# Induced attention with a running maximum in three of four batches, a one-product quadrant sum, and a rearranged first phase

## The chip, the cores and the metric

The kernel runs on one core of a Trainium2 chip. The metric is device time in microseconds for one execution. The kernel before has a median of 840.47 us over three runs (840.34 to 840.56).

Five engines matter. TensorE (PE in the profile; PEld is its weight load) multiplies and writes to the accumulator banks. VectorE (DVE) and ScalarE (ACT) read banks, compute elementwise and write to the on-chip memory. GpSimd (POOL) here does mostly one kind of subtraction. SyncE (SP) issues the transfers. Each engine works through its own instructions in the order in which they are written.

## The reference, cut to what matters

```python
B, N, m, C = 4, 12544, 32, 128          # batches, tokens, inducing points, channels
def mab(q, kv):                         # attention of q over kv
    s = scale * (q @ kv.transpose(0, 2, 1))
    a = np.exp(s - s.max(-1, keepdims=True))
    a /= a.sum(-1, keepdims=True) + 1e-09
    return a @ kv
h   = mab(inducing, x)                  # 32 x 128 per batch: "first attention"
y   = mab(x, h)                         # 12544 x 128 per batch: "second attention"
out = max(y @ w1, y @ w2, y @ w3) @ w_out   # 128 -> 768 -> 128, per token
```

All arrays are f32. The first attention reduces over all 12544 tokens of a batch, so h of a batch is known only after its last token.

## The kernel before, in words

A batch's 12544 tokens are 98 tiles of 128. They are worked in seven groups: group 0 has 2 tiles, groups 1 to 6 have 16 each. A full group is again four chunks of 512 tokens.

**First attention of a group.** `attend_products` (L265) forms the scores with the inducing points, 32 rows in each of four partition quadrants, in a bank. `attend_max` (L275), `attend_column` (L282), `attend_spread` (L289) and `attend_least` (L293) find the group's maximum per inducing point and leave its negative in column `gi` of `mneg`. `attend_weights` (L299) takes the exponential, with the row sums in column `gi` of `lst`. `attend_transpose` (L313) turns the weights, `attend_sums` (L323) multiplies them with the tokens, again in four column quadrants, and `attend_keep` (L336) copies the 128 x 128 result into slot `gi` of `hg`. So each group has its own maximum, and seven partial results lie in `hg`.

**Joining the groups.** After the last group `combine_least`, `combine_weights` and `combine_mask` (L401, L406, L411) make a weight per group; `combine_groups` (L422) multiplies each of the seven slots of `hg` by a masked selection matrix, which adds groups and quadrants; `sum_groups` and `total_sums` (L432, L434, L438) do the same for the sums of the exponentials; `invert_total` (L442, L443) and `combine_states` (L448) give `hT`, the scaled h.

**From h to the weights of the chunk loop.** Since y = p @ h (p are the second attention's weights), y @ w can be had as p @ (h @ w). U = h @ wcat, 32 x 1664, is formed once per batch. In batches 1 to 3 `combine_products` (L489) does this in two halves, each with 64 columns of TensorE twice; `combine_high` and `combine_low` split the result into a rounded part and its remainder, and `combine_rows` (L509) moves them with four transfers into the rows of `us`. In batch 0 `first_products`, `first_high` and `first_low` (L462, L467, L473 to L478) do it another way.

**The chunk loop.** A slot is one chunk and one of six 128-column blocks of the 768. `advance` issues pu (L605) and pv (L611) for a coming slot, the relu on ACT (L620), the rounded part hi on ACT (L627), the remainder lo on POOL or DVE (L635, L641) and the maximum h on DVE (L638). `stage2`, six slots behind, issues three products per slot into the accumulator (L661 to L663) and a fourth at a chunk's start (L660). A plain slot so has five TensorE products of 512 columns, and a window of 24 slots is one group.

**Order.** Everything is hand-ordered: each engine's instructions run in the order in which the Python statements issue them. The first attention and the second attention's scores (L524) of the next group or batch are put into the loop by a plan: `at(s, f)` calls f in slot s. In each window two `burst` calls, in slots 2 and 15, issue the quadrant products together. The first attention of batches 1 to 3 runs inside the chunk loop of the batch before. The first attention of batch 0 has nothing to hide under: it is `phase1_first`, into which the conversion of the weights is cut (`work(n)` takes n further steps of `convert`, L161 to L190, mostly on DVE; `WORK` says how many per group). Then the string `ORDER` sets the steps up to the chunk loop: a and b are softmax steps of the first two groups, a digit k is `first_high` of piece k, c is `first_low` of that piece, s is `advance`.

## Time and profile before

| what | value |
|---|---|
| median of three runs | 840.47 us |
| the profiled execution | 838.86 us, of it 837.0 us span, mean granted TensorE clock 0.996 |
| TensorE busy | 815.4 us, 97% of the span |
| ScalarE, VectorE, GpSimd busy | 741.9, 629.9, 635.3 us |
| TensorE busy, 0 to 50 us | 37.9 us |
| TensorE busy, 260 to 430 us (batch 1's loop) | 169.41 of 170 us |
| TensorE busy, 630 to 800 us (batch 3's loop, no first attention beside it) | 169.99 of 170 us |
| last TensorE product ends | about 833.4 us |

The span is from the first to the last instruction; the difference to the execution's own time lies around the program. Rows of the timeline give the start and the duration of an instruction or of a run of like ones (x8: eight of them); products are pipelined, so a product of 512 columns is listed with 0.39 us, while the next starts 0.23 us later. What an insertion costs is therefore read from starts, not from durations. An f32 product is two matmul instructions, a product in the rounded format is one. Idle time before an instruction, with what ended it, stands in square brackets.

### The profile page before, as it was taken

The numbers are of one execution on the slowest core, as the hardware profiler recorded it, in microseconds if no ns is written. First come the engines' busy times: TensorE is split into PE (matmuls) and PEld (weight loads), VectorE is DVE, ScalarE is ACT, GpSimd is POOL, SyncE is SP. The second block draws the span as 40 slices with busy tenths as digits, with TensorE's granted clock in tenths as the row PEclk, the third lists the DMA queues.
The fourth block names the chain that finished last, engine by engine and source line by source line (L and its number), as shares of the span: only waits on it lengthen the run. The fifth ranks groups of instructions, "written<-read, shape, count | busy, mean of one in ns | idle before, by whom it ended". The sixth has DMA issues, their size and how long they took to land.

```text
span 837.0 us, 14668 instructions
## 1 busy us (share of the span) xinstructions
PE 815.4 (97%) x4608; PEld 636.5 (76%) x4608; DVE 629.9 (75%) x1076; ACT 741.9 (89%) x1547; POOL 635.3 (76%) x512
## 2 busy tenths in 40 slices
PE   6879999999999999999999999999999999999998
PEld 4647777777788777877778778777778878778786
DVE  4958787778687777877777878777868778777864
ACT  5759898898799988988889989889879999999996
POOL 0049788787598787886878978878759888888887
PEclk9989999999999999999999999999999999999999
DMA  9823624433435345244333362431232222222221
GB/s 351 305 85 122 221 73 160 172 107 114 134 87 173 124 161 171 73 157 154 127 92 127 113 223 72 161 123 55 64 90 75 74 76 73 67 64 76 73 79 51
DMA packets 42717, 102.50 MB, mean 122 GB/s; under 512 B 8976, under 2 KB 11152, under 8 KB 37392
## 3 DMA queue, kind: packets, MB, share of 16 engines
q1 hardware_dynamic: 42640, 101.57, 37.4%
q8 instruction: 37, 0.61, 0.3%
q14 instruction: 40, 0.33, 0.1%
HBM read 48.12 MB, written 25.69 MB: 88 GB/s over the span
## 4 chain that ended last, share of the span: by engine, by line
PE 92%; DVE 1%; issue 0%; ACT 0%; DVEq 0%; ACTq 0%
PE acc L661 17%; PE pu L605 16%; PE pv L611 16%; PE acc L662 16%; PE acc L663 16%; PE acc L660 3%; PE aux L524 3%; PE acc L323 2%; PE aux L265 2%; PE aux L489 1%; PE aux L422 1%; DVE h L638 0%; PE acc L289 0%; DVE lo L641 0%; DVE rec L443 0%
## 5 line engine op out<-in xcount | busy, mean ns | idle before, releaser
L635 POOL TENSOR_TENSOR lo<-h,hi 128x512 fp32r<-128x512 f32 (+1 forms) x498 | 629.4, 1296 | 146.3 <-ACT hi L627 90.0
L638 DVE TENSOR_TENSOR h<-pv,ru 128x512 f32<-128x512 f32 (+1 forms) x600 | 404.4, 675 | 182.4 <-PE pv L611 117.1
L620 ACT ACTIVATE ru<-pu 128x512 f32<-128x512 f32 (+1 forms) x600 | 375.4, 626 | 66.8 <-PE pu L605 63.7
L627 ACT CAST hi<-h 128x512 fp32r<-128x512 f32 (+1 forms) x600 | 386.6, 644 | 0.3 <-DVE h L638 0.3
L661 PE MATMUL acc<-hi,wo_hi 128*128 128x512 f32 (+1 forms) x600 | 237.9, 396 | 0.0
L605 PE MATMUL pu<-pT,us 128*128 128x512 f32 (+1 forms) x600 | 233.2, 389 | 2.8 <-DVE us L473 1.0
L611 PE MATMUL pv<-pT,us 128*128 128x512 f32 (+1 forms) x600 | 233.3, 389 | 0.0
L662 PE MATMUL acc<-hi,wo_lo 128*128 128x512 f32 (+1 forms) x600 | 231.8, 386 | 0.0
L663 PE MATMUL acc<-lo,wo_hi 128*128 128x512 f32 (+1 forms) x600 | 231.6, 386 | 0.0
L661 PEld LDWEIGHTS acc<-hi,wo_hi 128*128 128x128 f32 x600 | 113.1, 188 | 43.0 <-issue 21.8
L605 PEld LDWEIGHTS pu<-pT,us 128*128 128x128 f32 x600 | 113.5, 189 | 26.2 <-POOL us L478 2.1
L611 PEld LDWEIGHTS pv<-pT,us 128*128 128x128 f32 x600 | 113.7, 189 | 23.6 <-DVE h L638 1.2
L663 PEld LDWEIGHTS acc<-lo,wo_hi 128*128 128x128 f32 x600 | 112.9, 188 | 23.0
L662 PEld LDWEIGHTS acc<-hi,wo_lo 128*128 128x128 f32 x600 | 113.0, 188 | 20.6
L641 DVE TENSOR_TENSOR lo<-h,hi 128x512 fp32r<-128x512 f32 x102 | 72.5, 711 | 0.8 <-ACT hi L627 0.8
L668 ACT COPY o<-acc 128x512 f32<-128x512 f32 (+1 forms) x100 | 61.6, 616 | 3.1 <-PE acc L663 3.1
L660 PE MATMUL acc<-pT,us 128*128 128x512 f32 (+1 forms) x100 | 38.9, 389 | 0.0
L221 POOL TENSOR_TENSOR wo_lo<-wf,wo_hi 128x768 fp32r<-128x768 f32 x1 | 1.8, 1817 | 40.5 <-ACT wo_hi L220 40.5
L323 PEld LDWEIGHTS acc<-xg,aT 128*32 128x32 f32 x768 | 20.4, 110 | 12.6 <-ACT ru L620 5.7
L265 PE MATMUL aux<-xT,iT 128*32 128x512 f32 x192 | 25.9, 596 | 2.1 <-ACT xT L257 2.1
L323 PE MATMUL acc<-xg,aT 128*32 128x128 f32 x768 | 25.8, 274 | 0.4
L524 PE MATMUL aux<-xT,hT 128*32 128x512 f32 x192 | 25.6, 604 | 0.0
(104 smaller groups left out, 438.2 us busy)
## 6 DMA issues: line engine op xcount, KB each, us to landing
out_dram<-o SPq DMA_DIRECT2D x96, 256.0 KB, 2.0
xg<-in_x_dram SPq DMA_DIRECT2D x23, 1024.0 KB, 6.9
xT<-in_xt_dram SPq DMA_DIRECT2D x18, 1024.0 KB, 5.6
pT<-ph SPq DMA_DIRECT2D x192, 64.0 KB, 2.0
pT<-pl SPq DMA_DIRECT2D x192, 64.0 KB, 2.0
raw<-in_w_dram SPq DMA_DIRECT2D x3, 768.0 KB, 12.1
us<-uh SPq DMA_DIRECT2D x6, 208.0 KB, 3.1
us<-ul SPq DMA_DIRECT2D x6, 208.0 KB, 3.7
```

The source lines that it names most:

```text
L323: nc.tensor.matmul(out=hps[q * M : (q + 1) * M, :C], lhsT=aT[:, t * M : (t + 1) * M], rhs=xg[:, t, :], start=(t < NQ), stop=(t + NQ >= nt),)
L605: nc.tensor.matmul(out=pu[:, :w], lhsT=state[c.b]["us"][:, 2 * j * P : (2 * j + 1) * P], rhs=c.pT[:, :w], start=True, stop=True)
L611: nc.tensor.matmul(out=pv[:, : d.w], lhsT=state[d.b]["us"][:, (2 * j + 1) * P : (2 * j + 2) * P], rhs=d.pT[:, : d.w], start=True, stop=True,)
L620: nc.scalar.activation(out=ru[:, :w], in_=pu[:, :w], func=AF.Relu)
L627: nc.scalar.copy(out=hi[:, : c.w], in_=h[:, : c.w])
L635: nc.gpsimd.tensor_sub(**args)
L638: nc.vector.tensor_max(out=h[:, : d.w], in0=pv[:, : d.w], in1=relus.pop(s)[:, : d.w])
L641: nc.vector.tensor_sub(**low)
L660: nc.tensor.matmul(out=c.acc[:, :w], lhsT=us[:, 2 * DF :], rhs=c.pT[:, :w], start=True, stop=False)
L661: nc.tensor.matmul(out=c.acc[:, :w], lhsT=wo_hi[:, j, :], rhs=c.hh[j][:, :w], start=False, stop=False)
L662: nc.tensor.matmul(out=c.acc[:, :w], lhsT=wo_lo[:, j, :], rhs=c.hh[j][:, :w], start=False, stop=False)
L663: nc.tensor.matmul(out=c.acc[:, :w], lhsT=wo_hi[:, j, :], rhs=c.hl[j][:, :w], start=False, stop=(j == NJ - 1))
```

## The change

1. **Running maximum and sums in batches 1 to 3.** `attend_least` takes the smaller of the group's column of `mneg` and the one before. The new `attend_scale` (ScalarE) makes the factor exp(old maximum - new maximum), `al`. The new `attend_add` (VectorE) does hs = hs * al + h, 128 x 128, and the same for the sums, 128 x 1. The copy into `hg` stays for group 0 only, and the weights, the mask and the seven-fold product go. Batch 0 keeps the way it had.
2. **One product for the quadrants.** `add_quadrants` is one f32 product of `hs` with the selection matrix, 32 columns, beside `total_sums`.
3. **U in four column groups at once.** `combine_products` is four products of 416 columns, each with 32 columns of TensorE, into one bank; there is one `combine_high` and one `combine_low` of 128 x 416, and `combine_rows` is sixteen transfers of 32 x 416, four at a time, three slots apart.
4. **Weighted sums last in a burst.** `attend_sums` is issued behind `attend_products`.
5. **First phase.** The inducing points' load is the first on the queue and their scaling the first on ScalarE; four conversion steps instead of two stand ahead of the loop over groups, and two fewer behind the last group's minimum; the w2 transposes and the products from them come one group earlier; the joining is written in another order; and `ORDER` has `c` earlier in two places.

```diff
-    WORK = ((2, 2), (2, 2), (2, 2), (3, 2), (3, 2), (0, 3))
-    ORDER = "a a a a b a a b 0 c m b a a b a b p b 1 s b b b c s S m b 2 s c s 3 c s"
+    WORK = ((2, 2), (2, 2), (2, 2), (3, 2), (3, 2), (1, 0))
+    ORDER = "a a a a b a a b 0 c m b a a b a b p b 1 s c b b b s S m 2 b s c 3 c s s"
 ...
     def attend_least(b, gi):
         nc.vector.tensor_reduce(out=st["mneg"][:, gi : gi + 1], in_=st["mp"][:, :NQ], axis=AX.X, op=ALU.min)
+        if b > 0 and gi > 0:
+            nc.vector.tensor_tensor(
+                out=st["mneg"][:, gi : gi + 1], in0=st["mneg"][:, gi : gi + 1], in1=st["mneg"][:, gi - 1 : gi], op=ALU.min
+            )
 ...
+    def attend_scale(b, gi):
+        st = state[b]
+        st["al"] = wk.tile([P, 1], F32, name="al", tag="al")
+        nc.scalar.activation(out=st["al"], in_=st["mneg"][:, gi - 1 : gi], func=AF.Exp,
+                             bias=st["mneg"][:, gi : gi + 1], scale=-1.0)
+    def attend_add(b, gi):
+        st = state[b]
+        if gi == 0:
 ...
+            nc.scalar.copy(out=st["hs"][:parts, :], in_=st["h"][:parts, :C])
+            st["l1"] = st["lst"][:, :1]
+            return
+        for total, new in ((st["hs"], st["h"][:, :C]), (st["l1"], st["lst"][:, gi : gi + 1])):
+            nc.vector.scalar_tensor_tensor(
+                out=total, in0=total, scalar=st["al"], in1=new, op0=ALU.mult, op1=ALU.add
+            )
+    def add_quadrants(st, bank):
+        st["sum"] = bank
+        nc.tensor.matmul(out=bank[:, :M], lhsT=st["hs"], rhs=sel[:, :M], start=True, stop=True)
 ...
     def phase1_first(weights):
         start_batch(0)
+        nc.sync.dma_start(out=iT, in_=ind_t)
+        nc.scalar.mul(out=iT, in_=iT, mul=scale)
         first_loads()
 ...
-        work(2)
+        work(4)
 ...
-            if gi == NG - 2:
+            if gi == NG - 3:
                 transpose_w2()
+            if gi == NG - 2:
+                prep_products()
 ...
+        attend_weights(0, NG - 1)
         attend_sums(0, NG - 2, bank_o[1])
         attend_keep(0, NG - 2)
-        attend_weights(0, NG - 1)
         combine_least(state[0])
         combine_weights(state[0])
         attend_transpose(0, NG - 1)
-        prep_products()
 ...
+    def combine_products(st, bank):
 ...
+        for k in range(NQ):
+            nc.tensor.matmul(out=bank[k * M : (k + 1) * M, :UQ], lhsT=st["hT"][:, :M],
+                             rhs=wcat[:, k * UQ : (k + 1) * UQ], start=True, stop=True)
 ...
-                    first += [(attend_sums, n, g - 1), (attend_products, n, g, bank_a[1])]
-                    at(s0 + 3, attend_keep, n, g - 1)
+                    first += [(attend_products, n, g, bank_a[1]), (attend_sums, n, g - 1)]
+                    at(s0 + 3, attend_add, n, g - 1)
 ...
-                    at(s0 + 10, combine_least, ("state", n))
-                    at(s0 + 11, combine_weights, ("state", n))
-                    at(s0 + 14, combine_mask, ("state", n))
-                    at(s0 + 16, attend_keep, n, g + 1)
-                    at(s0 + 15, sum_groups, ("state", n))
+                    at(s0 + 16, attend_add, n, g + 1)
+                    at(s0 + 18, add_quadrants, ("state", n), bank_a[1])
                     at(s0 + 18, total_sums, ("state", n), bank_a[0])
-                    at(s0 + 17, combine_groups, ("state", n), range(NG), bank_a[1])
                     at(s0 + 19, invert_total, ("state", n))
-                    at(s0 + 20, combine_states, ("state", n), 2)
-                    at(s0 + 21, combine_products, ("state", n), 0, bank_a[0])
-                    at(s0 + 21, combine_products, ("state", n), 1, bank_a[1])
+                    at(s0 + 19, combine_states, ("state", n), 1)
+                    at(s0 + 21, combine_products, ("state", n), bank_a[0])
 ...
+                    for r in range(NQ):
+                        at(s0 + 25 + 3 * r, combine_rows, ("state", n), r)
```

Three places of the order. First TensorE, where batch 1's groups are joined (hs is the running sum, sel the selection matrix, lst and l the sums of the exponentials). Before:

```order
L611 MATMUL pv_84<-pT,us 128x512
L422 MATMUL aux_80<-sw,hg 128x64 x7
L661 MATMUL acc_85<-hi,wo_hi 128x512
L662 MATMUL acc_85<-hi,wo_lo 128x512
L663 MATMUL acc_85<-lo,wo_hi 128x512
L605 MATMUL pu_82<-pT,us 128x512
L611 MATMUL pv_83<-pT,us 128x512
L438 MATMUL aux_79<-sel,l_2633 128x32
L660 MATMUL acc_86<-pT,us 128x512
```

Now, one slot later than the seven products stood:

```order
L639 MATMUL pu_82<-pT,us 128x512
L645 MATMUL pv_83<-pT,us 128x512
L372 MATMUL aux_80<-sel,hs 128x32
L477 MATMUL aux_79<-sel,lst 128x32
L694 MATMUL acc_86<-pT,us 128x512
```

Seven products of 64 columns have gone; one of 32 columns stands beside the one for the sums. U's products (L489 before, L524 now) stand three slots after L438 in both.

Second, VectorE at the end of batch 0's first attention (t, pw, rest, dst and wcat are conversion steps, mq and mneg the last group's maximum). Before:

```order
L275 TENSOR_REDUCE mq<-aux_79 128x1
L313 STREAM_TRANSPOSE aT<-a 128x512
L293 TENSOR_REDUCE mneg<-acc_85 128x1
L185 SCALAR_TENSOR_TENSOR dst<-size,rest 128x768
L190 TENSOR_TENSOR wcat<-dst,wf 128x6x128
L401 TENSOR_REDUCE mmin<-mneg 128x1
```

Now:

```order
L183 SCALAR_TENSOR_TENSOR dst<-size,rest 128x768
L188 TENSOR_TENSOR wcat<-dst,wf 128x6x128
L276 TENSOR_REDUCE mq<-aux_79 128x1
L319 STREAM_TRANSPOSE aT<-a 128x512
L294 TENSOR_REDUCE mneg<-acc_85 128x1
L440 TENSOR_REDUCE mmin<-mneg 128x1
```

The last two conversion steps stand ahead of the last group's maximum; two steps that stood behind group 1's maximum now stand ahead of it.

Third, ScalarE between the first attention and the chunk loop (uf is a copy from which POOL forms the remainder of piece 1 of U, ph the rounded weights of the first full group). Before:

```order
L467 CAST us<-acc_86 128x512
L620 ACTIVATE ru<-pu_81 128x256
L567 CAST ph<-aux_80 128x512
L477 COPY uf<-acc_86 64x512
L620 ACTIVATE ru<-pu_82 128x256
```

Now:

```order
L506 CAST us<-acc_86 128x512
L654 ACTIVATE ru<-pu_81 128x256
L516 COPY uf<-acc_86 64x512
L601 CAST ph<-aux_80 128x512
L654 ACTIVATE ru<-pu_82 128x256
```

The copy uf has moved ahead of ph.

More of the change, by code (lines that the diff above doesn't have):

```diff
@@ L106 @@
     iT = const.tile([P, M], F32, name="iT")
-    nc.sync.dma_start(out=iT, in_=ind_t)
     def load_raw(src):
@@ L141 @@
     nc.gpsimd.memset(eps, 1e-9)
-    nc.scalar.mul(out=iT, in_=iT, mul=scale)
     wf = xtp.tile([P, 2, DF], F32, name="wf", tag="xT")
@@ L478, in first_low @@
         nc.gpsimd.tensor_sub(out=us[low], in0=uf[low, :n], in1=us.bitcast(F32)[low])
[L481 to L488 removed]
+    def combine_products(st, bank):
+        st["us"] = bp.tile([P, UW], F32R, name="us", tag="us")
+        st["up"] = bank
+        for k in range(NQ):
             nc.tensor.matmul(
[L490 to L492 removed]
+                out=bank[k * M : (k + 1) * M, :UQ],
+                lhsT=st["hT"][:, :M],
+                rhs=wcat[:, k * UQ : (k + 1) * UQ],
                 start=True,
@@ L715, in softmax1 @@
         at(s + 8 + wait, attend_weights, b, gi)
+        if gi > 0:
+            at(s + 9 + wait, attend_scale, b, gi)
         at(s + 10 + wait, attend_transpose, b, gi)
```

83 lines of the change are left out of this document (41 added, 42 removed).

## The prediction

> **What bounds the kernel now.** First the page's busy times, then four stretches: the stall before the chunk loop (50 to 70 us), batch 1's loop, batch 3's loop.
>
> ```profile
> PE 815.4 (97%) x4608; PEld 636.5 (76%) x4608; DVE 629.9 (75%) x1076; ACT 741.9 (89%) x1547; POOL 635.3 (76%) x512
> ...
> 50.00:60.00 10.00, 5.88 (x27) 4.05 (x27) 6.45 (x14) 6.34 (x18) 3.99 (x6) 0.76 0.24 57
> 60.00:70.00 10.00, 10.00 (x56) 8.19 (x55) 8.32 (x15) 9.24 (x21) 7.84 (x8) 0.89 0.71 243
> 260.00:430.00 170.00, 169.41 (x990) 130.78 (x989) 128.40 (x219) 151.75 (x317) 132.82 (x105) 1.00 0.43 138
> 630.00:800.00 170.00, 169.99 (x778) 136.18 (x777) 134.81 (x223) 162.93 (x330) 144.63 (x116) 1.00 0.25 73
> ```
>
> The columns are length, then busy time of TensorE, its weight load, VectorE, ScalarE and GpSimd, the granted clock and DMA. In both loops TensorE is busy practically all the time. Batch 3's row has no first attention beside it; there ScalarE fills 162.93 of 170 us and TensorE still does not wait. So in batches 0 to 2, where ScalarE fills 151.75, a microsecond taken from TensorE should be a microsecond of the total. Before about 60 us it is otherwise: TensorE idles there, and waits decide.
>
> **U in four column groups.** The timeline's TensorE rows around U's products in batch 1's preparation, and around a burst of one kind in batch 3:
>
> ```profile
> 217.58 0.39 PE L611 MATMUL pv<-pT,us 128*128 128x512 f32 x1
> 218.42 1.62 PE L489 MATMUL aux<-wcat,hT 128*64 128x416 f32 x8 [0.45 <-DVE hT L448]
> 220.30 0.40 PE L662 MATMUL acc<-hi,wo_lo 128*128 128x512 f32 x1
> ...
> 686.23 0.39 PE L605 MATMUL pu<-pT,us 128*128 128x512 f32 x1
> 686.46 0.39 PE L611 MATMUL pv<-pT,us 128*128 128x512 f32 x1
> 686.77 1.06 PE L524 MATMUL aux<-xT,hT 128*32 128x512 f32 x8
> 688.11 0.39 PE L662 MATMUL acc<-hi,wo_lo 128*128 128x512 f32 x1
> ```
>
> A plain step is 0.23 us (686.23 to 686.46), and from L611 to L662 there are two, 0.46. The old insertion therefore costs 220.30 - 217.58 - 0.46 = 2.26 us, with the wait for hT in it. Eight matmul instructions in four column groups of 512 columns cost 688.11 - 686.46 - 0.46 = 1.19 with both changes of column width. The new ones have 416 columns; eight of 512 take 0.89 (124.08 to 124.97 below), so 96/512 of that, 0.17, comes off: 1.02. The saving is 1.24 per batch, 3.7 us for three. Bounds: 1.07 (no scaling) to 1.24, and 0.5 less if hT is late again. I take it as not late: the steps that make hT stand one slot earlier, and the mask (L411) ahead of them is gone. The Trainium skill's TensorEngine Tiling (Array Packing), section Theoretical Speedup, gives up to 2x for a dimension of 64 and 4x for 32; by that the 1.62 would become 0.81 and the saving would be about 0.1 us smaller per batch, which leaves the sum where it is within its bounds.
>
> **One product for the quadrants.**
>
> ```profile
> 210.97 0.39 PE L611 MATMUL pv<-pT,us 128*128 128x512 f32 x1
> 211.21 1.67 PE L422 MATMUL aux<-sw,hg 128*128 128x64 f32 x14
> 213.00 0.40 PE L662 MATMUL acc<-hi,wo_lo 128*128 128x512 f32 x1
> 213.70 0.39 PE L611 MATMUL pv<-pT,us 128*128 128x512 f32 x1
> 213.93 0.30 PE L438 MATMUL aux<-sel,l 128*128 128x32 f32 x2
> 214.38 0.39 PE L661 MATMUL acc<-hi,wo_hi 128*128 128x512 f32 x1
> ```
>
> The fourteen instructions cost 213.00 - 210.97 - 0.46 = 1.57 us, the sums' pair 214.38 - 213.70 - 0.46 = 0.22. Two such pairs side by side should cost 0.44 (bounds 0.22, if the second hides, to 0.9, if hs is late by what hT was). Saving 1.57 + 0.22 - 0.44 = 1.35 per batch, 4.0 us. hs is written in slot 16, on VectorE, and read in slot 18.
>
> **Weighted sums last.** The two burst forms, the transpose between them, and the weight loads' waits for the whole run:
>
> ```profile
> 92.50 1.07 PE L524 MATMUL aux<-xT,hT 128*32 128x512 f32 x8
> 92.78 0.71 DVE L313 STREAM_TRANSPOSE aT<-a 128x512 f32<-128x512 f32 x1
> 93.64 1.08 PE L323 MATMUL acc<-xg,aT 128*32 128x128 f32 x32
> ...
> 124.08 1.07 PE L524 MATMUL aux<-xT,hT 128*32 128x512 f32 x8
> 124.97 1.06 PE L323 MATMUL acc<-xg,aT 128*32 128x128 f32 x32
> ...
> PEld acc L323 <- ACT ru L620: 5.7, 6, 0.9
> ```
>
> At 92.50 the sums start 1.14 us after the scores, at 124.08 only 0.89: 0.25 is lost where aT ends at 93.49, just before they can start. The last row counts six such places (it names ScalarE, which had long been done; it is the transpose). With the products of about 0.87 between, aT is ready. That gives 1.5 us; bounds 0 (the wait appears elsewhere) and 1.5. Order inside a burst changes no other cost that these rows show.
>
> **What comes in its place, and its cover.**
>
> ```profile
> L448 DVE TENSOR_TENSOR hT<-pu,rec 128x128 f32<-128x128 f32 x1 | 0.3, 292 | 0.1
> L293 DVE TENSOR_REDUCE mneg<-acc 128x1 f32<-128x4 f32 x28 | 4.3, 153 | 1.2 <-PE acc L289 1.2
> 216.57 0.58 SPq L590 DMA_DIRECT2D pT<-pl  x1
> ```
>
> Per group, eighteen times in all, VectorE gets a 128 x 128 update from a bank (nearest 0.29), a 128 x 1 update and a 128 x 1 minimum (nearest 0.15 each): 0.6 us, at most 10.8 us altogether, while it idles 41.6 of 170 us in batch 1's loop. Behind them on VectorE stands the next h, for which POOL, ScalarE and pv's bank wait; the pipeline is six slots long, so I charge nothing. ScalarE exchanges a copy for a small exponential. SP issues sixteen transfers for U instead of four, about 0.58 each, 7 us more per batch in groups of four; behind them stand the p transfers of the next chunks. Their last four are issued in slot 34, and `us` is first read about thirteen slots (17 us at 1.3) later: hidden.
>
> So the loops give 3.7 + 4.0 + 1.5 = 9.2 us (bounds 6.5 to 9.9).
>
> **The first phase.** Rows of the timeline:
>
> ```profile
> 6.13 0.44 PE L265 MATMUL aux<-xTs,iT 128*32 128x64 f32 x8 [2.45 <-ACT iT L143]
> 13.09 0.69 DVE L275 TENSOR_REDUCE mq<-aux 128x1 f32<-128x512 f32 x1 [3.58 <-PE aux L265]
> 25.79 1.09 PE L255 MATMUL pu<-ident,xg 128*128 128x128 f32 x8 [0.68 <-DMA xg<-in_x_dram]
> 29.01 1.06 PE L265 MATMUL aux<-xT,iT 128*32 128x512 f32 x8
> 31.73 0.68 DVE L275 TENSOR_REDUCE mq<-aux 128x1 f32<-128x512 f32 x1
> 38.45 0.16 DVE L293 TENSOR_REDUCE mneg<-acc 128x1 f32<-128x4 f32 x1 [0.19 <-PE acc L289]
> 40.39 0.15 DVE L401 TENSOR_REDUCE mmin<-mneg 128x1 f32<-128x7 f32 x1
> 45.54 0.32 PE L524 MATMUL aux<-xTs,hT 128*32 128x64 f32 x8 [0.59 <-DVE hT L448]
> ...
> 53.03 0.58 ACT L567 CAST ph<-aux 128x512 fp32r<-128x512 f32 x1 [0.91 <-DVE aux L564]
> 53.64 0.58 ACT L477 COPY uf<-acc 64x512 f32<-64x512 f32 x1
> 54.27 0.49 PE L462 MATMUL acc<-wcat,hT 128*128 128x128 f32 x2 [1.34 <-ACT uf L477]
> 55.61 0.58 PE L605 MATMUL pu<-pT,us 128*128 128x256 f32 x1 [0.85 <-POOL us L478]
> ```
>
> The earlier load of iT takes up to 2.45 us out of the start, but group 5's tokens arrive at 25.79, and TensorE had waited 0.68 for them already: most of the gain is spent in a longer wait there. What remains is VectorE's lateness. Group 5's scores end at 30.07, its maximum starts at 31.73; two conversion steps moved into the hole of 3.58 let VectorE be on time: 1.5 us, less about 0.4 because one more step now stands between groups 5 and 6, and 0.2 for arrival: 0.9 (bounds 0 to 1.5). Then mmin started 1.94 us after the last group's minimum, with two steps between; it now follows at once, but the exponential and transpose of the last group are next late, so I take 1.4 (bounds 0 to 1.94). Third, uf goes ahead of ph, which waited 0.91: it gains about 1.5, TensorE's wait of 1.34 goes, POOL's remainder and with it L605 come 1.5 sooner, and the second `c` moved helps a little: 1.8 (bounds 0, if the next wait takes it all, to 2.1). First phase 4.1, bounds 0 to 5.5.
>
> Sum: 9.2 + 4.1 = 13.3. The profiled execution took 838.86, which becomes 825.6 (span 837.0 to about 823.7); the median of the runs is 840.47, which becomes **827.2**.
>
> **Rivals.**
>
> *The first phase gives almost nothing*: data arrive as before, and the waits between 46 and 60 us close up differently. 25.79 with its wait speaks for it; the 3.58 hole and ph's wait against. 840.47 - 9.2 = 831.3.
>
> *The granted clock stays up.* In 50 to 70 us the clock averages 0.76 and 0.89, which is 2.4 + 1.1 = 3.5 us of TensorE time. It falls after idle stretches (5.88 busy of 10). If the shortened waits keep it at 1.00, up to 3 us more come: 840.47 - 13.3 - 3 = 824.2. Against it: waits of about 1 us remain there. The Trainium skill, TensorE: Matmul & The Clock Gate, section What's actually happening, says that a window of about 3.4 us judged idle halves the clock and that the window runs freely; by that the outcome depends on where the waits fall in it, and a longer low stretch is as possible as none.
>
> *ScalarE sets the pace after all* in batches 0 to 2, and TensorE's savings become its idle time: only the first phase counts, 840.47 - 4.1 = 836.4. Batch 3's row speaks against it.
>
> *VectorE's running update costs a slot.* The update stands in VectorE's queue between two h; if the next pv must wait for h there, each of eighteen groups loses time. It decides from 13.3/18 = 0.74 us per group on; at a whole slot, 1.3 us, it costs 23.4: 840.47 - 13.3 + 23.4 = 850.6. Against it stand VectorE's idle quarter and the six slots.
>
> That the change does not do what it says is excluded by the order of the instructions: the fourteen are gone, the column groups are there.
>
> **How the numbers follow.** The forecast gets 0.60, the empty first phase 0.14, the clock 0.13, ScalarE's pace 0.08, VectorE's slot 0.05. The range 823 to 832 holds the first three and the bounds of the sum; above it lie the last two. A measurement of this kernel can tell 0.2% (1.7 us) from no change. Faster by more: 0.92; within: 0.03; slower: 0.05.
>
> **What would show it.** Right: no L489-like wait for hT, U's insertion near 1.0 us and the joining near 0.44 from start to start, no wait of the sums' weight loads, the last minimum of batch 0 near 37.5, and the scores L524 near 43.2. Wrong: TensorE idle for h or ru in batches 0 to 2, a new wait for `us` at a batch's start, or a gain in the first phase that is gone again by 62 us.

## The result, and the profile after

The kernel after takes 834.85 us (median of four runs, 834.19 to 836.23), the kernel before 840.51 beside it (840.34 to 840.72). The ratio is 0.9935, with a 95% interval of 0.9917 to 0.9952. So it is 5.7 us faster where 13.3 were forecast: the direction holds, the size does not, and the time lies above the range.

The page of after, then the same stretches as before in the view of windows (length, then busy time of TensorE, weight load, VectorE, ScalarE, GpSimd, the granted clock, DMA):

```profile
PE 813.4 (98%) x4572; PEld 632.0 (76%) x4572; DVE 648.9 (78%) x1115; ACT 743.7 (89%) x1541; POOL 637.0 (76%) x512
...
50.00:60.00 10.00, 6.44 (x29) 3.72 (x30) 7.03 (x16) 7.34 (x21) 5.25 (x6) 0.89 0.19 46
60.00:70.00 10.00, 10.00 (x51) 8.06 (x50) 7.21 (x13) 8.11 (x19) 7.10 (x7) 0.77 0.74 244
260.00:430.00 170.00, 169.40 (x983) 130.29 (x976) 134.95 (x234) 153.46 (x317) 135.17 (x106) 1.00 0.42 136
630.00:800.00 170.00, 169.29 (x774) 135.48 (x773) 134.18 (x219) 162.27 (x329) 144.03 (x115) 1.00 0.25 73
```

TensorE has 36 instructions less, and VectorE is busy 19 us longer (648.9 against 629.9), where the forecast had at most 10.8. Batch 1's loop looks as full as before: busy time of TensorE does not show what follows, because a product whose successor is late is listed as running on (0.48 us in a row below, where 0.39 is usual). The question is asked better with starts. The eleventh slot's first product and the last slot's lie here, in before and in after (timeline, TensorE):

```profile
63.79 0.40 PE L605 MATMUL pu<-pT,us 128*128 128x512 f32 x1
826.91 0.39 PE L605 MATMUL pu<-pT,us 128*128 128x512 f32 x1
```
```profile
64.53 0.41 PE L639 MATMUL pu<-pT,us 128*128 128x512 f32 x1
823.89 0.39 PE L639 MATMUL pu<-pT,us 128*128 128x512 f32 x1
```

I call the stretch between them "the loops": 763.12 us before, 759.36 after. They gained 3.8 us of the 9.2 in the forecast. In the two profiled executions the first phase lost 0.7 (63.79 to 64.53), although the medians leave it a gain of about 1.9 (5.7 less 3.8). That 1.9 is a remainder and not a measurement: the first phase differs from run to run, the profiled execution of after is the slowest of its four (836.23), and the interval of the ratio alone is 1.5 us either way.

Yet the three savings in the loops are there. Timeline of after, TensorE, around the joining, around U, and a burst:

```profile
213.28 0.39 PE L645 MATMUL pv<-pT,us 128*128 128x512 f32 x1
213.51 0.30 PE L372 MATMUL aux<-sel,hs 128*128 128x32 f32 x2
213.65 0.39 PE L477 MATMUL aux<-sel,lst 128*128 128x32 f32 x2
213.87 0.48 PE L694 MATMUL acc<-pT,us 128*128 128x512 f32 x1
...
217.37 0.39 PE L645 MATMUL pv<-pT,us 128*128 128x512 f32 x1
217.69 0.91 PE L524 MATMUL aux<-wcat,hT 128*32 128x416 f32 x8
218.86 0.39 PE L696 MATMUL acc<-hi,wo_lo 128*128 128x512 f32 x1
...
93.25 1.06 PE L558 MATMUL aux<-xT,hT 128*32 128x512 f32 x8
94.14 1.04 PE L266 MATMUL aux<-xT,iT 128*32 128x512 f32 x8
94.99 1.06 PE L329 MATMUL acc<-xg,aT 128*32 128x128 f32 x32
```

The two pairs cost 213.87 - 213.28 - 0.23 = 0.36 (forecast 0.44), U 218.86 - 217.37 - 0.46 = 1.03 (forecast 1.02), and in the burst the sums follow the products after 0.85, with no wait for aT. Slot by slot, the starts of pu in after and before differ by these amounts at these places: 1.38 us per batch for joining, 1.24 for U, 0.26 twice per batch for the transpose. That is 9.4 us. Something else in the loops takes 5.6 back.

The view of waits of after names one that before does not have, three times 0.9 (line waited for, total us, times, longest); and the timeline shows one of the three, on VectorE, then GpSimd, then TensorE:

```profile
DVE lo L675 <- PE acc L697: 2.7, 3, 0.9
...
258.83 1.51 DVE L672 TENSOR_TENSOR h<-pv,ru 128x512 f32<-128x512 f32 x2 [0.25 <-PE pv L645]
261.28 1.60 DVE L675 TENSOR_TENSOR lo<-h,hi 128x512 fp32r<-128x512 f32 x1 [0.94 <-PE acc L697]
...
261.03 1.30 POOL L669 TENSOR_TENSOR lo<-h,hi 128x512 fp32r<-128x512 f32 x1 [1.75 <-ACT hi L661]
...
260.32 0.29 PE L266 MATMUL aux<-xTs,iT 128*32 128x64 f32 x8
260.89 0.28 PE L697 MATMUL acc<-lo,wo_hi 128*128 128x256 f32 x1
```

VectorE's subtraction waits for TensorE's third product, which *reads* a lo, of another slot. That looks like a wait for memory: the tiles of hi, lo and h take whatever place is free at that time, and this change brings other tiles. The subtraction is that of slot 156, and the product it waits for is slot 152's, issued just here behind the burst's scores; so in after the place of a lo is written again four slots later. In before the subtraction began at 261.69, ahead of slot 152's product (262.33), so its place must have had an earlier reader. The traces hold no addresses; the experiments below test it. Having waited, the subtraction starts 0.25 us behind GpSimd's and takes 1.60 us; in before it took 0.68:

```profile
261.69 0.68 DVE L641 TENSOR_TENSOR lo<-h,hi 128x512 fp32r<-128x512 f32 x1
```

The other suspects are VectorE's new instructions. The groups of after (count | total us, mean ns | idle before):

```profile
L366 DVE SCALAR_TENSOR_TENSOR lst<-lst,al 128x1 f32<-128x1 f32 x18 | 9.5, 528 | 0.0
L297 DVE TENSOR_TENSOR mneg<-mneg 128x1 f32<-128x1 f32 x18 | 6.1, 340 | 0.6
L366 DVE SCALAR_TENSOR_TENSOR hs<-hs,al,acc 128x128 f32<-128x128 f32 x18 | 5.7, 318 | 0.0
```

The two updates of a single column, forecast at 0.15 us each, take 0.53 and 0.34 on average, more than the 128 x 128 update next to them.

### The profile page after: what moved, and what is told of

Same layout as the page of the kernel before. It is cut to its first block, busy times and chain, and to the rows that moved or that the text cites. A ratio compares the mean times of both kernels' runs of the same rounds, so it can differ in the third digit from the quotient of the medians.

```text
span 834.1 us, 14694 instructions
## 1 busy us (share of the span) xinstructions
PE 813.4 (98%) x4572; PEld 632.0 (76%) x4572; DVE 648.9 (78%) x1115; ACT 743.7 (89%) x1541; POOL 637.0 (76%) x512
## 4 chain that ended last, share of the span: by engine, by line
PE 93%; DMA 3%; DVE 2%; ACT 1%; SPq 0%; issue 0%; POOL 0%; ACTq 0%; DVEq 0%
PE acc L695 17%; PE pu L639 16%; PE acc L696 16%; PE pv L645 16%; PE acc L697 16%; PE aux L558 3%; PE acc L694 3%; DMA xg<-in_x_dram 3%; PE acc L329 2%; PE aux L266 2%; DVE h L672 0%; ACT ru L654 0%; PE acc L290 0%; ACT hi L661 0%; DVE aux L571 0%
## 5 line engine op out<-in xcount | busy, mean ns | idle before, releaser
L675 DVE TENSOR_TENSOR lo<-h,hi 128x512 fp32r<-128x512 f32 x102 | 77.7, 762 | 5.5 <-PE acc L697 2.7
L266 PE MATMUL aux<-xT,iT 128*32 128x512 f32 x192 | 25.3, 598 | 1.6 <-ACT xT L258 1.6
```

What stands on the lines that cost most here:

```text
L675: nc.vector.tensor_sub(**low)
```

## The experiments

The theories for the loops were: the three waits for lo's memory cost about 1 us each; and VectorE's new instructions, or ScalarE's factor `al`, hold the next h back. The rival to both: the savings themselves are smaller than they look. For the first phase: the order of its steps gives what was forecast and the granted clock takes it back; or it gives nothing.

All timed results, each against the kernel before in the same series (its medians 839.0 to 840.2); "loops" is the stretch defined above, from the profiled execution:

| run | median us | ratio (95%) | loops us |
|---|---|---|---|
| rot_before | 840.59 | 1.0011 (1.0000-1.0022) | 763.1 |
| rot_loops | 832.24 | 0.9922 (0.9908-0.9937) | 756.6 |
| rot_first | 838.81 | 0.9989 (0.9978-1.0000) | 763.1 |
| rot_after | 832.24 | 0.9915 (0.9902-0.9929) | 756.6 |
| lo_short | 840.61 | 1.0013 (1.0003-1.0024) | 764.0 |
| lo_share | 843.35 | 1.0035 (1.0022-1.0048) | 766.0 |
| no_factor | 830.31 | 0.9881 (0.9861-0.9902) | 755.4 |
| fill_loops | 832.16 | 0.9907 (0.9891-0.9924) | 756.6 |
| fill_after | 830.03 | 0.9884 (0.9870-0.9899) | 756.6 |
| fill_loads | 829.70 | 0.9881 (0.9864-0.9898) | 756.4 |
| best_1 | 829.98 | 0.9881 (0.9864-0.9897) | 756.4 |
| warm_loops | 834.11 | 0.9932 (0.9919-0.9946) | 756.5 |
| warm_after | 830.18 | 0.9886 (0.9869-0.9903) | 756.6 |
| best_2 | 829.60 | 0.9881 (0.9866-0.9895) | 756.6 |
| best_3 | 827.17 | 0.9855 (0.9830-0.9880) | 754.1 |

Three more have a profile and a single time: no_update (830.32 us, loops 755.9), no_both (830.50, 755.8), sums_first (834.42, 758.2).

### Fixed memory for h, hi and lo

In all four kernels these tiles rotate through fixed places, so that the distance of re-use is the same whatever else is allocated. rot_before is the kernel before with this alone, rot_after the whole change, rot_loops has the change's loops with the old first phase, rot_first the reverse. In these kernels' rows max, high and low stand for h, hi and lo.

```diff
+    lows = [const.tile([P, 512], F32R, name=f"low{i}") for i in range(6)]     # maxs: 5, highs: 6
-            lo = hp.tile([P, 512], F32R, name="lo", tag="lo", bufs=10)
+            lo = lows[(s - 1) % len(lows)]
```

> The kernel before, with the remainders lo, the maxima h and the rounded parts hi in six, five and six fixed tiles used in rotation, instead of tiles that the program's memory planner places anew for each use. A control. Theory A (the planner's re-use of lo, which came one or two uses sooner in the changed kernel, costs time at each batch's start): lo already came round after six uses in the kernel before, so nothing changes, 840.5 us, within 0.8. Theory B (the re-use does not matter; the running update on VectorE and the sixteen transfers themselves hold up h): also 840.5. Were it faster by more than 1.5 us, the planner's placing would cost time in the kernel before as well, and the other three runs would have to be read against this one.

> The changed chunk loops with the first phase (and ORDER) of the kernel before, with lo, h and hi in fixed tiles in rotation. In the traces the three loop terms gained 1.38 + 1.25 + 0.52 = 3.15 us per batch, 9.4 in all, and 1.0 per batch was lost at a batch's start, about 0.5 around the second bursts, 0.4 in small pieces. Theory A (re-use of lo): the 1.0 is gone, so 840.5 - 9.4 + 2.7 = 833.8 us. Theory B (the update or the transfers): the 1.0 stays, 836.8.

> The kernel before with the changed first phase (and ORDER) alone, with lo, h and hi in fixed tiles in rotation. Theory C (data arrival at about 26 us and the granted clock behind it eat what the reordering saves): 839.5 to 841.5 us, with runs that differ by 1 to 2 us. Rival D, the prediction's own term: 4.1 less, 836.4.

> The whole change, with lo, h and hi in fixed tiles in rotation. Theory A: 834.9 less 1.0 at each of three batch starts, 831.8 us, and VectorE's lo no longer waits for TensorE. Theory B: 834.8, and the step at a batch's start stays 1.0 us longer than in the kernel before.

The rotation does nothing to the kernel before (loops 763.1 in both) and takes 2.8 us from the changed loops (759.4 to 756.6). The three waits are gone from rot_after's groups; its ends and VectorE's lo:

```profile
62.43 0.39 PE L642 MATMUL pu<-pT,us 128*128 128x512 f32 x1
818.98 0.39 PE L642 MATMUL pu<-pT,us 128*128 128x512 f32 x1
...
L678 DVE TENSOR_TENSOR low<-max,high 128x512 fp32r<-128x512 f32 x102 | 73.9, 724 | 0.8 <-ACT high L664 0.8
```

In after the same group had 77.7 us and 2.7 of waits for TensorE. The loops so give 6.5 us of their 9.4, and the new first phase gives 1.8 us with the old loops (840.59 to 838.81) but none with the new (832.24 both). Executions of one of these kernels lie up to 1.7 to 3.8 us apart, so 1.8 and 0 are not clearly different.

### The wait for lo alone

The converse: rot_before, with the six slots concerned sharing one tile, so that each second one must wait for the reader four slots earlier.

```diff
+    SHORT = (152, 156, 302, 306, 452, 456)
+            lo = shared if (s - 1) in SHORT else lows[(s - 1) % len(lows)]
```

> The converse: the kernel before with the fixed rotation (run rot_before), but the remainder lo of the first full slot of batches 1, 2 and 3 (slots 156, 306, 456, VectorE's own) shares one tile with the remainder four slots earlier, as the planner laid it in the changed kernel; nothing else of the change is in it. Theory A (this re-use is what costs 1.0 us at a batch's start): the products behind those slots come 1.0 us later each time, 3.0 us in all, 0.36% slower than rot_before; VectorE's lo waits about 0.9 us for TensorE there and then takes about 1.6 instead of 0.68. Theory B (the running update or the transfers): no change.

In lo_short the second write stands ahead of the product that reads the first, in the order of the statements, so it is TensorE that waits for the new lo, and no subtraction for a reader: the steps are 0.27, 0.27 and 0.38 us. It does not pose the question. lo_share issues the three subtractions behind that slot's products, as after has them in effect:

```diff
+        if low and s - 2 in SHORT:
+            pipe["late"] = low           # issued behind stage2 of this slot
```

> The converse again, now rightly ordered: run rot_before, but the remainder lo of slots 156, 306 and 456 (the first full slot of batches 1 to 3, on VectorE) has the same tile as the remainder of four slots earlier, and is written only after TensorE's third product of that earlier slot has read it, as in the changed kernel. In lo_short the write stood ahead of that read, so that TensorE waited and not VectorE, and the product read the wrong remainder. Theory A: VectorE's lo waits about 0.9 us there and takes about 1.6 beside POOL instead of 0.68, and the products behind come 1.0 us later three times, 3.0 us in all (0.36%). Theory B: below 0.3 us each, as in lo_short.

Waits and timeline of lo_share, VectorE:

```profile
DVE shared L826 <- PE acc L670: 2.7, 3, 0.9
...
264.56 1.59 DVE L826 TENSOR_TENSOR shared<-max,high 128x512 fp32r<-128x512 f32 x1 [0.94 <-PE acc L670]
```

Wait and slowed subtraction are those of after, within 0.01 us. The starts of pu fall behind by 1.01, 1.01 and 0.82 us at these three places and nowhere else (the third after 0.3 is gained back a few slots on); the loops take 766.0 instead of 763.1. So re-using one tile after four slots, where the rotation leaves six, costs 1 us a time, and 2.9 in all. **Shown both ways.** (How much of the 1 us is the wait and how much the slow subtraction was not separated.)

The doubling from 0.68 to 1.60 fits a rule of the Trainium skill (SBUF — State Buffer, section SBUF: two separate sides): a VectorE instruction with two operands in on-chip memory and a GpSimd instruction that reads it share a port pair, and the second stands still until the first has ended. GpSimd's row of after above ends at 262.33, VectorE's 0.55 us behind it, though it had started only 0.25 behind. The trace agrees: all 16 of VectorE's lo subtractions in after that took over 0.8 us ended 0.55 or 0.56 us behind the GpSimd subtraction that was running when they started.

### VectorE's column updates and ScalarE's factor

Three variants of rot_after: no_factor puts a constant 1 for `al` (no exponential on ScalarE, sums not rescaled), no_update leaves out both updates (sums not accumulated), no_both does both.

```diff
-            at(s + 9 + wait, attend_scale, b, gi)
+            at(s + 9 + wait, attend_one, b, gi)          # no_factor: al = 1.0
-        for total, new in ((st["hs"], st["h"][:, :C]), (st["l1"], st["lst"][:, gi : gi + 1])):
+        for total, new in ():                            # no_update
```

> The run rot_after without the small exponential on ScalarE that makes the factor al; a constant 1 takes its place, so the sums are not rescaled when the maximum moves. VectorE's update stays. Theory F (the exponential stands ahead of the relu on ScalarE in the two crowded windows of a batch): the steps of +0.30 at slots 94 and 95 and of +0.27 at slots 118 and 119 of each batch go, 0.55 to 0.7 per batch, 1.7 to 2.1 us in all: 831.4 where rot_after stands at 833.3 (0.9915 of 840.5). Rival G (VectorE's update costs it): the steps stay, 833.3.

> The run rot_after without VectorE's running update: hs and the sum keep group 0's values, so the first attention is not summed; the exponential al on ScalarE stays. In the trace of no_factor 0.10 at slots 95 and 119 of each batch and 0.05 per window are left of the loops' losses, about 0.5 us per batch. If VectorE's update is their cause, they go here (TensorE's slots stand 0.5 us per batch earlier against rot_after). If the order inside the bursts (scores ahead of weighted sums) is the cause, they stay.

> The run rot_after without the factor and without the running update (hs and the sum keep group 0's values). From the first chunks on (slot 10 to the last), rot_after's loops are 6.5 us shorter than the kernel before's, while the three terms that were forecast came to 9.4: 2.9 are lost. Without the factor alone 1.16 of them come back, without the update alone 0.70. If the two are the whole cause and simply add, 1.9 come back here; if they stand in each other's way on VectorE and ScalarE, up to 2.9; what is then left is the order of the bursts or a thing not seen yet.

The loops give back 1.2, 0.7 and 0.8 us. They do not add up, because removing the updates shifts what is left: in no_update and no_both the minimum of the two crowded windows of a batch (slots 90 and 114) falls beside a GpSimd subtraction and takes 0.99 us, where in rot_after it took 0.16, and pv then waits 0.43 for the late maximum, a wait that rot_after does not have there. The minimum in no_both:

```profile
166.93 0.99 DVE L297 TENSOR_TENSOR mneg<-mneg 128x1 f32<-128x1 f32 x1
```

What the updates do in the change itself is read from rot_after: first one update and the wait behind it, then a wait in a crowded window, then the weight loads' waits for the whole run.

```profile
96.30 2.55 POOL L672 TENSOR_TENSOR low<-max,high 128x512 fp32r<-128x512 f32 x2 [1.87 <-PE pu L642]
96.92 0.70 DVE L366 SCALAR_TENSOR_TENSOR lst<-lst,al 128x1 f32<-128x1 f32 x1
97.54 0.68 DVE L675 TENSOR_TENSOR max<-pv,ru 128x512 f32<-128x512 f32 x1
98.27 0.19 PEld L648 LDWEIGHTS pv<-pT,us 128*128 128x128 f32 x1 [0.18 <-DVE max L675]
...
172.12 0.19 PEld L642 LDWEIGHTS pu<-pT,us 128*128 128x128 f32 x1 [0.41 <-ACT ru L657]
...
PEld pv L648 <- DVE max L675: 3.5, 18, 0.4
PEld pu L642 <- ACT ru L657: 3.2, 7, 0.8
```

The column update takes 0.70 us beside GpSimd, the next maximum is late, and pv waits 0.18 for it: pv's bank is free only when that maximum has read it. This is the forecast's "next h", which the six slots did not cover. It happens four times per batch. But the larger loss takes another way. Behind a late maximum ScalarE's hi is late, and then its relu, which starts 0.93 us after pu's product instead of 0.50 (before) and stays as late for the slots that follow. In the two crowded windows of a batch, where in before too the relu falls to 1.2 us and more behind, that is too late for pu's bank: pu waits 0.41 for it. By starts of pu, these six waits cost about 0.27 us each, 1.6 in all; the other 0.9 goes with the twelve of pv.

The test that separates this from ScalarE's factor changes only the form of the two column updates. With the second column given as a scalar per partition, each has one on-chip tensor operand instead of two. It stands on best_2, which is described below and has rot_after's loops (756.6):

```diff
-            nc.vector.tensor_tensor(out=m_gi, in0=m_gi, in1=m_before, op=ALU.min)     # names shortened
+            nc.vector.tensor_scalar(out=m_gi, in0=m_gi, scalar1=m_before, scalar2=None, op0=ALU.min)
-            nc.vector.scalar_tensor_tensor(out=l1, in0=l1, scalar=al, in1=l_gi, op0=ALU.mult, op1=ALU.add)
+            nc.vector.tensor_scalar(out=l1, in0=l1, scalar1=al, scalar2=l_gi, op0=ALU.mult, op1=ALU.add)
```

> The run best_2 with VectorE's 128 x 1 minimum and 128 x 1 sum written with one tensor from the on-chip memory and per-partition scalars, instead of two tensors from there. In the changed kernel's trace they take 0.34 and 0.53 us on average (0.16 to 0.51, 0.21 to 0.70) where the forecast took 0.15 from a reduction, and they are long where POOL's subtraction runs beside them. If it is the second tensor from the on-chip memory that waits for POOL, they fall to about 0.15 and 0.2, the next h comes sooner, and about half of what no_update and no_both point to comes back, 0.3 us per batch: 828.7 us against 829.6. If they wait for something else, they stay as long and so does the kernel.

Groups, waits and ends of best_3:

```profile
L372 DVE TENSOR_SCALAR lst<-lst,al 128x1 f32<-128x1 f32 x18 | 4.8, 266 | 0.0
L300 DVE TENSOR_SCALAR mneg<-mneg 128x1 f32<-128x1 f32 x18 | 3.9, 214 | 0.6
...
PEld pv L672 <- DVE max L699: 1.3, 6, 0.4
PEld pu L666 <- ACT ru L681: 0.8, 1, 0.8
...
60.92 0.40 PE L666 MATMUL pu<-pT,us 128*128 128x512 f32 x1
815.02 0.39 PE L666 MATMUL pu<-pT,us 128*128 128x512 f32 x1
```

The same arithmetic takes 0.27 and 0.21 us instead of 0.54 and 0.38 (best_2), twelve waits of pv and six of pu are gone, and the loops take 754.1 us, 2.5 less than best_2's: 9.0 of the 9.4. The gain is larger than was expected of it. The factor, still there in best_3, thus costs at most the remaining 0.4; what no_factor gave back was room on ScalarE, which the late updates had taken (pu's six waits are 0.25 there). The rule named above fits here too. Of the 36 column instructions of after, 27 took 0.26 to 0.70 us, and all 27 ended 0.01 to 0.03 us behind the GpSimd subtraction that was running when they started; in best_3 all 36 take 0.21 to 0.27, wherever they fall. The 128 x 128 update, the same instruction with its second operand in a bank, kept 0.32 us in every kernel.

sums_first is rot_after with the burst's order put back:

```diff
-                    first += [(attend_products, n, g, bank_a[1]), (attend_sums, n, g - 1)]
+                    first += [(attend_sums, n, g - 1), (attend_products, n, g, bank_a[1])]
```

> The run rot_after with the weighted sums ahead of the scores in the bursts again, as in the kernel before: one part of the change undone. The prediction's term: 0.25 us at each of six places comes back, +1.5 us, so TensorE's slots at the end stand 1.5 us later than in rot_after. If the order inside the bursts is also what costs the 0.2 to 0.3 us per batch that neither the factor nor the update explains, only 0.6 to 0.9.

The starts fall behind by 0.26 or 0.27 us at six places, and nowhere else: the forecast's term for the late transpose, whole.

### The first phase

Intervals of the first phase, worked out from the starts in the timelines (last minimum of batch 0; from there to the second attention's scores, L524 in before; from there to the seventh slot's first product; from there to the eleventh's):

| kernel | last minimum at | to scores | to slot 6 | to slot 10 |
|---|---|---|---|---|
| before | 38.45 | 7.08 | 13.31 | 4.95 |
| rot_loops (old order) | 38.35 | 7.08 | 13.31 | 4.91 |
| after | 40.26 | 5.97 | 12.16 | 6.14 |
| rot_after (new order) | 38.41 | 5.97 | 12.13 | 5.92 |
| fill_after | 38.19 | 5.97 | 13.43 | 3.45 |
| best_2 | 39.39 | 5.84 | 12.15 | 3.44 |
| no_factor | 38.28 | 5.97 | 12.13 | 3.45 |

The last column says where a gain went. The kernels with filled idle time, described below, take 3.44 or 3.45 us there in the new order, at full clock. So does no_factor, whose profiled execution kept the full clock without any filling: it took 827.43 us, its other three 830.21 to 831.30. Two windows (clock last but two) for before, rot_after and fill_after:

```profile
54.00:58.00 4.00, 1.90 (x7) 1.44 (x8) 1.76 (x4) 2.50 (x8) 2.22 (x3) 0.66 0.34 82
58.00:62.00 4.00, 4.00 (x14) 3.54 (x15) 2.38 (x6) 2.94 (x8) 3.19 (x5) 0.50 0.70 184
```
```profile
54.00:58.00 4.00, 2.64 (x8) 2.03 (x9) 2.55 (x6) 2.76 (x10) 2.84 (x4) 0.66 0.41 100
58.00:62.00 4.00, 4.00 (x21) 2.88 (x20) 1.76 (x4) 2.94 (x7) 1.47 (x2) 0.50 0.87 275
```
```profile
54.00:58.00 4.00, 2.92 (x16) 2.31 (x17) 2.84 (x7) 2.97 (x10) 2.33 (x4) 1.00 0.35 84
58.00:62.00 4.00, 4.00 (x32) 3.27 (x31) 3.27 (x6) 3.90 (x9) 2.13 (x4) 1.00 0.49 94
```

Before and rot_after have half the clock until the same time, about 62 us. In rot_after the slots come sooner, but more of them run at half pace: 21 products in four microseconds, where fill_after has 32. In after's own profile the clock is at half from 57.7 to 64.5 and also from 27.0 to 30.4, which is why its last minimum (40.26) and its last column look worse than before's. fill_after is rot_after with twenty products of 256 columns, whose result nobody reads, put in where TensorE idles between 47 and 56 us; fill_loops is rot_loops with 27 such.

```diff
-    ORDER = "a a a a b a a b 0 c m b a a b a b p b 1 s c b b b s S m 2 b s c 3 c s s"
+    ORDER = "a a a a b a a b 0 c f3 m b a a b a b p b f6 1 s c b b b s S m f5 2 b s c 3 c s f6 s"   # fn: n products
```

> The run rot_after with twenty extra products of 256 columns (0.12 us each, into columns of an accumulator bank that nobody reads) in the places between 47 and 56 us where TensorE waits, so that TensorE is not idle there. Theory C (the low granted clock, half from 54.7 to 62.2 us in the kernel before, eats what the first phase saves): the clock stays at 1.0 through 50 to 65 us, the 3.5 us of TensorE time that the low clock costs are saved, less up to 0.5 for the products: 830 us. Rival: the clock falls anyway or the waits grow by the same amount, 833.

> The run rot_loops (first phase of the kernel before) with such extra products in its waits between 47 and 58 us. With the clock held in both, its difference to the run fill_after is what the rearranged first phase is worth by itself: the prediction said 4.1 us; theory C says 1.5 to 2.5 (group 6's tokens and the waits behind uf), so 831.5 to 832.5 us here against 830 there. If the clock is not what eats the gain, this run equals rot_loops, 834.

fill_after gains 2.2 us on rot_after, fill_loops nothing on rot_loops (832.16 and 832.24). With the idle stretches filled in both, the new first phase is worth 2.1 us on the medians, where the plain pair gave 0. The profiles bear the 2.1 out: from the last minimum to the eleventh slot it is 23.6 us in fill_loops and 21.6 in no_factor, both at full clock. At half clock it is 25.3 (rot_loops) and 24.0 (rot_after), so the old form loses 1.7 there and the new one 2.5, as it has more slots there. In fill_after's own profile a half-clock stretch from 44.5 to 47.9, ahead of most of its filling, costs 1.3 us again (13.43 in the third column). The Trainium skill (TensorE: Matmul & The Clock Gate, section What's actually happening) has a free-running window of about 3.4 us which halves the clock if judged idle; the half stretches of after, 27.0 to 30.4 and 57.7 to 64.5, are 3.4 and 6.8 us long and agree.

Is the forecast's first term lost to the arrival of group 5's tokens? fill_loads is fill_after with these tokens ahead of the last piece of the weights on the queue.

```diff
-    LOADS = (0, 7, 1, 2, 8, 3, 9, 4, 10, 5, 6)
+    LOADS = (0, 7, 1, 2, 8, 3, 9, 4, 5, 10, 6)
```

> The run fill_after with group 5's tokens loaded ahead of the last weight instead of behind it. They were awaited for 1.4 us at 26 us. If their arrival sets the first phase's pace, the last group's minimum comes 1 to 1.4 us earlier and so does all behind it: 828.8 us where fill_after has 830.0. If VectorE sets it (in rot_after it has no gap from 22 to 37 us, with five conversion steps a group), the minimum moves by less than 0.3 us: 830.0.

Nothing changes (829.70 against 830.03, and the intervals between the groups' minima agree within 0.2 us). What sets the pace there is VectorE itself (rot_after, timeline):

```profile
26.31 0.70 DVE L319 STREAM_TRANSPOSE aT<-a 128x512 f32<-128x512 f32 x1
26.93 0.92 DVE L179 TENSOR_TENSOR rest<-rest,t 128x768 f32<-128x768 f32 x1
27.88 0.96 DVE L183 SCALAR_TENSOR_TENSOR dst<-size,rest 128x768 f32<-128x768 f32 x1
28.88 0.96 DVE L188 TENSOR_TENSOR wcat<-dst,wf 128x768 f32<-128x768 f32 x1
```

From 22 to 37 us it has no gap. The two steps moved to the start came from behind the last group, so the work between the groups is what it was, and one step more stands ahead of the last group's minimum.

Four kernels change more of the first phase: best_1 is fill_after with the conversion of the output weights moved behind the last exponential on ScalarE and 16 products of 128 columns between 39 and 45 us; warm_after and warm_loops are fill_after and fill_loops with 27 such products between 2 and 11 us as well as those 16; best_2 is warm_after with the moved conversion.

```diff
+        prep_out()                      # best_1, best_2: wo_hi's conversion, behind attend_weights(0, NG - 1)
+        warm(12, bank_o[1])             # warm_*, best_2: idle products at the start
```

> The run fill_after with extra products of 128 columns in TensorE's waits from 2 to 11 us (27 of them) and from 39 to 45 us (16). In the profiled executions TensorE starts at half pace (eight transposes in 1.95 us instead of 1.09) and comes to full pace at about 11 us in some and at about 15 us in others; VectorE waits for it there and has no gap afterwards until the last group's maximum, whose minimum ends at 38.2 us in the first kind and at 40.2 in the second. If idle TensorE at the start is what makes the full pace late, it comes by 11 us in every execution: 829.0 us with less spread than fill_after's 829.6 to 830.7, and the last minimum at 38.2 or earlier. If the pace does not depend on it, 830 as in fill_after.

> The run fill_loops (first phase of the kernel before) with the same extra products. With TensorE's pace the same in both, its difference to warm_after is the worth of the rearranged first phase by itself. The prediction said 4.1 us (0.9 + 1.4 + 1.8). The traces say: last minimum 0 to 0.4 earlier (VectorE's queue sets it), minimum to scores 1.1 to 1.3, behind that 0.7 to 0.8 (slot 2 comes 1.5 sooner, of which 0.8 is given back at slot 6, which waits for the transfers of p): 2.0 to 2.5 us, so 831.2 here if warm_after is at 829.0.

> The run warm_after with ScalarE's conversion of w_out moved behind the last group's exponential, for which it stood 0.3 to 0.9 us in the way. If that exponential is on the path, 828.6 us; if the waits behind it (uf, the transfers of p) take it up, 829.0 as warm_after.

They lie within 0.4 us of fill_after where they have the new order; warm_loops is 2 us worse than fill_loops (in its profile the clock is at half from 40.2 to 43.6, and the scores come 9.02 us after the last minimum instead of 7.08). For the warm pair 829.0 and 831.2 had been expected, for best_2 828.6. The warm pair gives 3.9 us for the new first phase, but its profiles differ by 2.8 at the eleventh slot. Their last minima lie at 41.2 (warm_after), 40.0 (warm_loops) and 39.4 (best_2). Without products at the start the last minimum lies at 38.2 to 38.7 in some profiles and at 39.9 to 40.3 in the others, by when TensorE comes to its full pace (after, with its half clock at 27 us, is the exception). Two rows of the start, rot_after and rot_first, the same eight products:

```profile
11.48 1.07 PE L266 MATMUL aux<-xT,iT 128*32 128x512 f32 x8 [0.68 <-ACT xT L258]
```
```profile
11.42 1.93 PE L263 MATMUL aux<-xT,iT 128*32 128x512 f32 x8 [0.68 <-ACT xT L255]
```

In some executions the full pace begins at about 11 us, in others at about 15. The clock records of a trace begin there too: at 9.8 to 12.9 us in the thirteen traces where these products take 1.06 or 1.07 us, and at 15.4 to 16.5 in the seven where they take 1.93 or 1.94. Ahead of its first record a window shows 1.00 for want of one, so the late start looks like a half clock that is held longer. The early products did not settle which of the two it is (warm_after's profile has the late kind, warm_loops' and best_2's the early). What decides it **stays open**; together with the half-clock stretches later on, which also differ from one execution to the next, it would explain why runs of one kernel differ by 1 to 2 us. The moved conversion shortened only the second column, 5.97 to 5.84.

## Why the prediction was right or wrong

**U, joining, weighted sums last: right**, 3.7, 4.1 and 1.6 us measured by starts against 3.7, 4.0 and 1.5. (Two side workings there do not come out, though the sum does not use them: if the 1.62 became 0.81 (it became 0.91), U would save 0.81 us per batch, or 1.26 with the wait of 0.45 gone, not 0.1 less than 1.24; and the lower bounds named add up to 3.2 + 2.7 + 0 = 5.9, not 6.5. The 3.8 measured lies below both.) hT was not late, the second pair of the joining hides more than assumed, and `us` was never waited for at a batch's start.

**"What comes in its place, and its cover" failed**, at "I charge nothing". It cost 5.6 us of the 9.4, in two parts.

1. The waits for lo's memory, 2.8 to 2.9 us (rot_after, lo_share). The prediction has no term for them: they come from where tiles fell in memory, which neither the diff nor a row of before tells. What could have warned is that a lo's place is used again a few slots after its reader, and that the burst stands just ahead of one reader.
2. The column updates, 2.5 us (best_3). I took 0.15 us each from a row whose operand lies in a bank; with two on-chip operands they took 0.34 and 0.53. They made the next h late, and this reached TensorE in two ways: pv waited for h twelve times (0.9 us), and ScalarE, late with hi, was late with the relu, for which pu waited six times (1.6 us). "TensorE idle for h or ru in batches 0 to 2" stood among the signs of being wrong, and both came. "VectorE idles 41.6 of 170 us" was no cover, as an idle quarter on average says nothing about the 1.3 us of one slot.

So the rival of VectorE's update costing a slot named a wait that exists, pv for h, but it is the smaller of the two, and all of it comes to about 0.14 us per group on average (2.5 / 18), far from the 0.74 from which the rival decides.

**First phase, 4.1 forecast; about 1.9 left by the medians, with a wide margin.** By term: "0.9, VectorE on time" was nothing that can be told from zero (last minimum at 38.2 to 38.7 in the old order and 38.2 to 38.5 in the new, in profiles with the early start and no half clock before it): the moved steps came from behind the last group, and the hole of 3.58 lies ahead of a stretch in which VectorE, without a gap, is the pace. "1.4, mmin at once" was 1.1 (7.08 to 5.97); of what is missing, the conversion of wo_hi that stands in the exponential's way on ScalarE is 0.13 (5.84 in best_2). "1.8, uf ahead of ph" was 1.2 at the seventh slot (13.31 to 12.13), and of it about 1.0 is gone again by the eleventh (4.95 to 5.92), at half clock. That was named among the signs of being wrong, a gain "gone again by 62 us", but not priced. So the profiles give 1.3 to the eleventh slot (25.34 to 24.02), and with idle time filled the new first phase is worth 2.1 as a whole.

**The rivals.** The empty first phase (831.3) is the nearest, though for another reason than it gave: arrival changes nothing (fill_loads), and the loops lost as well. The clock that stays up came by itself in one of 27 executions with the new first phase and no filling (no_factor's 827.43, 2.8 to 3.9 below its other three, where 3 were assumed); in the change's own four it fell. Made to stay, it brought 2.2 us (fill_after). ScalarE does not set the pace of the loops, as best_3 has 9.0 of the 9.4; but in two windows of a batch its relu came too late, and there TensorE waited for it.

The sum, then: 9.4 in the loops, less 2.8 for lo's memory and 2.9 for the updates and what little remains, is 3.7; the 1.9 for the first phase is what is missing to the 5.7 measured, so that the sum closes proves nothing about it. best_3, which mends all three, takes 827.17 us (826.9 to 828.91; ratio 0.9855, 0.9830 to 0.9880), the lowest median. That it stands where the forecast for the change had stood is luck: it gets there with filled idle time, which was no part of the forecast.

## What to carry to other kernels

Where TensorE is full and its neighbours are hand-timed, price a new small VectorE instruction that reads two tensors from on-chip memory by the GpSimd instruction that may run beside it (0.70 and 0.99 us here), not by its size; better, give it the form with one such tensor. A delay on one engine can also reach TensorE through the next: follow it there. Where tiles are placed by a planner, any new tile may shorten the re-use distance of others: look for new waits of a writer for a reader, and fix the rotation by hand if one lies on the path. And a gain ahead of a stretch at half clock can be lost in it, if the clock returns no sooner (1.2 us became 0.2 here).

## What the runs showed of the hardware that was not expected

- A VectorE instruction on one column of 128 values took 0.99 us beside GpSimd's subtractions (1.3 us each), and a 128 x 512 subtraction 1.60 instead of 0.68; the same column operations with a scalar per partition took 0.21 and 0.27 us on average instead of 0.38 and 0.54. The 27 slow column instructions of after all ended within 0.03 us of a GpSimd subtraction's end.
- TensorE's full pace begins at about 11 us in some executions and at about 15 in others (eight products in 1.07 or 1.93 us); the trace's clock records begin only then, and the 1.00 that windows show ahead of them is no record.
- Twenty products without use, in idle time, took 2.2 us from the median (rot_after to fill_after): the half-clock stretch at 55 to 62 us was gone. One execution without them (no_factor) kept the full clock as well.
